# Early attention of a fused attention and two-FFN kernel: features taken from transposed queries, memory and normaliser in one product, and GpSimd given two elementwise jobs

## The chip, the cores and the metric

The kernel runs on one core of a Trainium2 chip. A core has TensorE (PE in the profile, with its weight loads on PEld), VectorE (DVE), ScalarE (ACT), GpSimd (POOL) and SyncE (SP), each with its own instruction queue, executed in order. Time is device microseconds (us) of one execution; three runs of the kernel before give a median of 1062.53 us.

## The reference

Causal attention over 4 batches of 8 heads (576 tokens, 64 columns a head) is mixed by a gate with a read from a linear memory; two feed-forward networks (FFNs) follow.

```python
a = softmax(causal(q @ k.T / sqrt(64)))            # per batch b and head h
local = a @ v
q_p = where(q > 0, q, exp(q) - 1) + 1              # the feature
mem_out = (q_p @ M_prev) / (q_p @ z_prev + 1e-6)
g = 1 / (1 + exp(-beta))
x = g * mem_out + (1 - g) * local                  # 2304 tokens x 512
h = x @ w_in                                       # 512 x 2048, layer 0
y = (max(h, 0) + log1p(exp(-abs(h)))) @ w_out
h = y @ w_in2                                      # layer 1
out = where(h > 0, h, exp(min(h, 0)) - 1) @ w_out2
```

## The kernel before

Tokens are cut into five chunks (`CHUNKS`) of 512 to 416. A chunk goes through layer 0 and then layer 1 in `ffn`: 16 steps f (a column block of 128 of the hidden layer), then 4 output blocks of 4 steps. Each fp32 product is made from two parts, a rounded high part and the rest as a low part (`hi`, `lo`; columns 0 and 1 of `x` and `g`), in three matmuls: hi x hi, hi x lo, lo x hi (L598 to L600 and L614 to L616). `convert` turns one raw 512 KB weight block into such a pair: ACT scales the upper words (L528), DVE shifts and joins the lower ones (L529, L530), ACT casts to the high part (L97, `w<-wr`), DVE subtracts to get the low part (L539). Raw blocks come through SP's queue into three buffers (tag `big`).

Attention is a generator. Part "A" is the first 256 tokens of a batch, part "B" the other 320; each is run head pair by head pair (4 pairs). A pair p of part "A" does: products of keys and queries (L294), mask and minimum on DVE (L333), exponentials on ACT (L338), the row scales on DVE (L348), transposes of the result (`group`, L373) and a copy to SBUF (L97, `pt<-tp`), and in `gather_pair` the product with the values (L407), summed in the PSUM bank `o` with the memory read (L404). `into` moves `o` into x: a cast on ACT (L142) and the low part on DVE (L143).

The memory read needs the feature. `feature` makes it with tokens on the partitions: exp (L241) and q+1 (L242) on ACT, then on DVE minimum and maximum (L243), a product with z (L244), a sum over the 64 columns (L246), gate and reciprocal (L249, L250) and the division (L252). `feature_t` transposes it on TensorE (L261) and ACT copies it back (L97, `phi<-tp`), so that L404 can multiply with M.

Part "A" of batches 0 and 1 fills chunk 0 and comes first, together with the first 14 weight blocks of layer 0 (`make(..., True)`); I call this the opening. Layer 0 of chunk 0 cannot begin before `x` of pair 0 of batch 1 is there. Afterwards `order` of `TUNE` says how many attention and conversion steps are called between FFN steps; parts "A" of batches 2 and 3 come first there. The order of instructions on each engine is decided when the program is built, by a scheduler with priorities, and is then fixed.

Of the kernel before, what the change touches and what calls it, by code (L numbers as in the profile page):

```python
# [23 lines left out]
TOK = ((128, 128), (0, 128), (512, 64), (384, 128), (256, 128))  # L24
# [34 lines left out]
def kernel(  # L59
# [32 lines left out]
    def f32(ap):  # L92
        return ap.bitcast(F32)
# [13 lines left out]
    iomg = const.tile([128, H], F32, name="iomg")  # L107

    def constants():
# [13 lines left out]
        ve.reciprocal(iomg, iomg)  # L123

# [20 lines left out]
    def attention(b, part, pool, early=None):  # L145
# [3 lines left out]
        cols = (1, 0) if first else (4, 3, 2)  # L149
# [16 lines left out]
        def load_kq(p):  # L166
# [3 lines left out]
            t = two.tile([128, 960], F32, name="kq", tag="kq")  # L170
# [12 lines left out]

        def load_rest(p):
            if first:
                if early:
                    for key in "qzvm":
                        d[key, p] = early[key][p]
                    return
                else:  # L190
                    t = (two if p % 2 else pool).tile([128, 6, 128], F32, name="ar", tag="ar")
                    ge.dma_start(t[:, 0:2, :], qz[b, p, :, 0:2, :])
                    ge.dma_start(t[:, 2, :], qz[b, p, :, 5, :])
                    ge.dma_start(
                        t[:, 3:5, :].rearrange("p h (t c) -> p h t c", t=2),
                        vm[b, p, :, 0:10, :].rearrange("p (h t) c -> p h t c", h=2)[:, :, 0:2, :],
                    )
                    ge.dma_start(t[:, 5, :].rearrange("p (h c) -> p h c", h=2), vm[b, p, :, 10:12, :])
                d["q", p], d["z", p] = t[:, 0:2, :], t[:, 2:3, :]
                d["v", p] = t[:, 3:5, :].rearrange("p h (t c) -> p h t c", t=2)  # L200
                d["m", p] = t[:, 5, :].rearrange("p (h c) -> p h c", h=2)
# [36 lines left out]
        def feature(p):  # L238
            q, z = d.pop(("q", p)), d.pop(("z", p))
# [15 lines left out]
        def feature_t(p):  # L255
            e = d.pop(("e", p))
# [6 lines left out]
            if plain:  # L263
                phi = two.tile([128, CB], F32, name="phi", tag="phi")
                copy(E[T["eva"][0]], phi[:, :n], pt[:, :n])
                d["phi", 2 * p] = d["phi", 2 * p + 1] = phi
                return
# [131 lines left out]
        def gather_pair(n):  # L399

            p = n // 2
            o = pso.tile([128, 512], F32, name="o", tag="o")
            for h in range(2):
                te.matmul(o[own(h), :w], d["vs", n + h][0][own(h)], d["phi", n + h][own(h), :w], start=True, stop=False)  # L404
            for j, p0, pn in ((0, 0, 256), (1, 256, 128)):
                for h in range(2):
                    te.matmul(o[own(h), :pn], d["vs", n + h][1][:, j, :], d["pt", n + h][0][:, p0:p0 + pn],  # L407
# [21 lines left out]
        if first:  # L429
            load_rest(1)  # L430
            load_rest(2)
        feature(0)
        prep_v(0)
        yield
        for p in range(NP if first else 0):
# [5 lines left out]
            if p + 2 < NP:  # L441
                load_kq(p + 2)
            yield
            if p:
                group(n - 2, d["pt", n - 2][0], ((1, 0), (0, 0), (1, 1)))
# [335 lines left out]
```

## Time and profile before

| what | before |
|---|---|
| median of 3 runs | 1062.53 us (1062.15 to 1063.73) |
| the profiled execution | 1062.3 us, span of its trace 1060.5 us |
| TensorE busy | 1029.0 us (97%) |
| DVE, ACT busy | 683.3 us (64%), 668.6 us (63%) |
| GpSimd busy | 91.4 us (9%) |

The span runs from the first to the last instruction; the 1.8 us between it and the execution's time lie outside the trace. TensorE's 97% is an average: its idle time is almost all in the first 90 us.

### The profile page before, as it was taken

Reading aid. Unit: us, or ns where it says so; the run is one execution under the profiler, and the core shown is the slowest. Engines: PE = TensorE matmul, PEld = TensorE weight load, DVE = VectorE, ACT = ScalarE, POOL = GpSimd, SP = SyncE. Lnnn points to the kernel's source line nnn. Section 1 sums busy time; section 2 is a strip of 40 time slices with the busy share of each in tenths; the row PEclk is TensorE's granted clock in tenths of the full one; section 3 lists DMA queues with packets and bytes.
Section 4 is the critical chain, followed back from the end, with each engine's and each line's share of the span. In section 5 each row is a group of like instructions: output and inputs, shape, how many; then the busy total and the mean of one; then the engine's idle time right before and its main releaser. Section 6 shows DMA issues by size and latency. Waiting matters only on the chain.

```text
span 1060.5 us, 15777 instructions
## 1 busy us (share of the span) xinstructions
PE 1029.0 (97%) x5328; PEld 904.7 (85%) x5328; DVE 683.3 (64%) x1698; ACT 668.6 (63%) x1458; POOL 91.4 (9%) x173
## 2 busy tenths in 40 slices
PE   7589999999999999999999999999999999999998
PEld 5356677788888888888889999999999999999998
DVE  6967799666768997897567756964675370240540
ACT  6759896697668977676569845654894350470330
POOL 7213330000000001000000000000000000000000
PEclk9989999999999999999999999999999999999999
DMA  9694489998976699646566466567545578777675
GB/s 284 185 367 147 149 274 329 336 332 293 336 279 246 220 311 343 207 165 193 198 228 235 170 233 217 178 231 241 194 162 176 182 247 246 247 234 233 231 235 174
DMA packets 73120, 251.65 MB, mean 237 GB/s; under 512 B 10320, under 2 KB 14928, under 8 KB 73040
## 3 DMA queue, kind: packets, MB, share of 16 engines
q1 hardware_dynamic: 64432, 216.56, 59.5%
q0 software_dynamic: 8608, 34.09, 10.1%
q8 instruction: 42, 0.69, 0.3%
q14 instruction: 38, 0.31, 0.1%
HBM read 212.34 MB, written 38.27 MB: 236 GB/s over the span
## 4 chain that ended last, share of the span: by engine, by line
PE 85%; DVE 6%; DMA 5%; ACT 2%; issue 1%; SPq 0%; ACTq 0%; DVEq 0%; POOLq 0%
PE h L614 12%; PE h L616 12%; PE h L615 12%; PE h L598 11%; PE h L600 11%; PE h L599 11%; PE tp L373 5%; PE o L388 2%; PE s L298 2%; PE h L298 2%; PE o L389 1%; PE o L407 1%; DMA w<-in_w1i 1%; PE s L294 1%; DVE wr L530 1%
## 5 line engine op out<-in xcount | busy, mean ns | idle before, releaser
L598 PE MATMUL h<-x,w 128*128 128x512 f32 (+2 forms) x640 | 238.5, 377 | 5.5 <-DVE t L577 2.3
L599 PE MATMUL h<-x,w 128*128 128x512 f32 (+2 forms) x640 | 239.6, 374 | 0.0
L600 PE MATMUL h<-x,w 128*128 128x512 f32 (+2 forms) x640 | 239.2, 374 | 0.0
L614 PE MATMUL h<-g,w 128*128 128x512 f32 (+2 forms) x640 | 238.4, 373 | 0.1
L616 PE MATMUL h<-g,w 128*128 128x512 f32 (+2 forms) x640 | 237.6, 372 | 0.0
L615 PE MATMUL h<-g,w 128*128 128x512 f32 (+2 forms) x640 | 237.3, 371 | 0.0
L598 PEld LDWEIGHTS h<-x,w 128*128 128x128 f32 x640 | 120.6, 189 | 21.1 <-DVE t L577 2.8
L600 PEld LDWEIGHTS h<-x,w 128*128 128x128 f32 x640 | 120.8, 189 | 13.4 <-issue 0.8
L599 PEld LDWEIGHTS h<-x,w 128*128 128x128 f32 x640 | 120.8, 189 | 12.5 <-issue 0.7
L614 PEld LDWEIGHTS h<-g,w 128*128 128x128 f32 x640 | 120.3, 188 | 12.8 <-issue 0.6
L616 PEld LDWEIGHTS h<-g,w 128*128 128x128 f32 x640 | 120.3, 188 | 11.9 <-issue 1.1
L615 PEld LDWEIGHTS h<-g,w 128*128 128x128 f32 x640 | 120.3, 188 | 11.7 <-issue 0.8
L603 DVE TENSOR_TENSOR g<-t,g 128x512 fp32r<-128x512 f32 (+2 forms) x160 | 101.0, 634 | 33.0 <-ACT g L602 31.5
L602 ACT CAST g<-t 128x512 fp32r<-128x512 f32 (+2 forms) x160 | 91.4, 573 | 24.6 <-DVE t L585 19.2
L321 ACT ACTIVATE sph<-sph,neg 128x384 f32<-128x384 f32 (+2 forms) x96 | 67.4, 702 | 31.9 <-DVE neg L315 31.4
L577 DVE SCALAR_TENSOR_TENSOR t<-h,t 128x512 f32<-128x512 f32 (+2 forms) x80 | 50.6, 636 | 57.2 <-ACT t L576 56.9
L379 DVE TENSOR_TENSOR ptb<-tp,ptb 128x512 fp32r<-128x512 f32 (+2 forms) x96 | 53.0, 575 | 38.2 <-ACT ptb L378 37.8
L378 ACT CAST ptb<-tp 128x512 fp32r<-128x512 f32 (+2 forms) x96 | 44.9, 498 | 46.4 <-PE tp L373 45.9
L373 PE MATMUL tp<-ident,sph 128*128 128x128 f32 x480 | 72.3, 282 | 1.5 <-ACT phi L97 1.1
L373 PEld LDWEIGHTS tp<-ident,sph 128*128 128x128 f32 x480 | 59.8, 145 | 9.8 <-ACT phi L97 1.5
L528 ACT ACTIVATE wr<-w 128x512 f32<-128x512 f32 x64 | 42.8, 669 | 35.0 <-DMA w<-in_w2i 11.7
L584 ACT ACTIVATE t<-t 128x416 f32<-128x416 f32 (+2 forms) x64 | 36.8, 579 | 41.4 <-DVE t L583 38.1
(117 smaller groups left out, 1535.3 us busy)
## 6 DMA issues: line engine op xcount, KB each, us to landing
w<-s_1i SPq DMA_DIRECT2D x79, 512.0 KB, 4.1
w<-s_0i SPq DMA_DIRECT2D x64, 512.0 KB, 4.2
w<-s_0o SPq DMA_DIRECT2D x64, 512.0 KB, 4.2
w<-s_1o SPq DMA_DIRECT2D x64, 512.0 KB, 4.2
qk<-in_qk POOLq DMA_DIRECT2D x32, 480.0 KB, 5.4
w<-in_w1i SPq DMA_DIRECT2D x16, 512.0 KB, 4.5
s_0i<-w SPq DMA_DIRECT2D x16, 512.0 KB, 7.0
w<-in_w1o SPq DMA_DIRECT2D x16, 512.0 KB, 5.3
```

What stands on the lines that cost most here:

```text
L321: se.activation(Pi, Pi, ACTF.Exp, scale=-1.0, bias=neg[:, i:i + 1], accum_out=sums(n, i))
L373: te.transpose(pt[:, c:c + 128], P[:, poff(n, i) + 128 * j:poff(n, i) + 128 * j + 128], ident)
L379: ve.tensor_sub(dst[:, 1, :c], pt[:, :c], f32(dst)[:, 0, :c])
L577: ve.scalar_tensor_tensor(t, h, 0.0, t, ALU.max, ALU.add)
L598: te.matmul(h[:, :N], hi[:, k, :], xk[:, 0, :N], start=k == 0, stop=False)
L599: te.matmul(h[:, :N], hi[:, k, :], xk[:, 1, :N], start=False, stop=False)
L600: te.matmul(h[:, :N], lo[:, k, :], xk[:, 0, :N], start=False, stop=k == KD - 1)
L602: se.copy(g[:, 0, :N], t[:, :N])
L603: ve.tensor_sub(g[:, 1, :N], t[:, :N], f32(g)[:, 0, :N])
L614: te.matmul(h[:, :N], hi[:, k, :], gs[f][:, 0, :N], start=f == 0, stop=False)
L615: te.matmul(h[:, :N], hi[:, k, :], gs[f][:, 1, :N], start=False, stop=False)
L616: te.matmul(h[:, :N], lo[:, k, :], gs[f][:, 0, :N], start=False, stop=f == KF - 1)
```

## The change

Batch parts "A" alone change; parts "B" and the FFNs keep their code.

- The feature is made from the transposed queries that lie beside the keys in `kq` already, for both heads of a pair at once, with no transpose ahead: exp on ACT, q+1 on GpSimd for batches 0 and 1 (`L258` of the new file) and on ACT for 2 and 3, minimum and maximum on DVE.
- One product per 128 tokens (L285) multiplies the feature with a 128 x 130 tile `mz`: M of both heads on the diagonal and two columns of z. Its PSUM result holds the memory read and the normaliser, tokens on the partitions. DVE adds, inverts (L289, L290) and scales (L292) it into `e`; `gather_pair` transposes `e` straight into the sum `o` (L438) ahead of the values' products.
- z comes once for all batches (`zc`, by one load and a transpose), M once a batch (`load_memory`); the per-pair loads of q, z and M fall away, and the values alone remain (one load a pair in place of four).
- The low part of the 14 early weight blocks is made by GpSimd (`ge.tensor_sub`) in place of DVE.
- The first three raw weight loads are issued between the first attention loads on SP's queue (`fetch`), and `kq` of pairs 2 and 3 of batch 1 gets buffers of its own.
- The two early 128-token tiles are stored in natural order, which only permutes rows and columns.

```diff
+    zc = const.tile([128, B * NP, 2], F32, name="zc")
...
+        nc.gpsimd.dma_start(zrow, qz[:, :, 0, 5, :].rearrange("b p c -> (b p) c"))
+        ge.memset(zc, 0.0)
+        te.transpose(zt[:, 0:B * NP], zrow, ident[0:B * NP, 0:B * NP])
+        for h in range(2):
+            ve.tensor_copy(zc[64 * h:64 * h + 64, :, h], zt[64 * h:64 * h + 64, 0:B * NP])
...
+        def load_memory():
+            t = pool.tile([128, NP, 130], F32, name="mz", tag="mz")
+            ge.memset(t, 0.0)
+            for h in range(2):
+                ge.dma_start(t[own(h), :, 64 * h:64 * h + 64], vm[b, :, own(h), 10 + h, :].rearrange("p r c -> r p c"))
+            ge.tensor_copy(t[:, :, 128:130], zc[:, b * NP:b * NP + NP, :])
...
         def feature(p):
+            if first:
+                q = d["kq", p][:, CA:2 * CA]
+                se.activation(e, q, ACTF.Exp)
+                if b < 2:
+                    ge.tensor_scalar(phi, q, 1.0, None, ALU.add)
+                else:
+                    se.activation(phi, q, ACTF.Identity, bias=ones)
+                ve.scalar_tensor_tensor(phi, e, 1.0, phi, ALU.min, ALU.max)
...
         def feature_t(p):
+            if first:
+                am = pss.tile([128, 512], F32, name="tp", tag="s")
+                for i in range(2):
+                    te.matmul(am[:, 130 * i:130 * i + 130], phi[:, 128 * i:128 * i + 128], d["mz"][:, p, :], start=True, stop=True)
+                ve.scalar_tensor_tensor(nrm, am[:, :, 128:130], 1e-6, g2, ALU.add, ALU.mult)
+                ve.reciprocal(nrm, nrm)
+                ve.tensor_mul(e, am, nrm.rearrange("p t (h o) -> p t h o", o=1).to_broadcast([128, 2, 2, 64]))
...
         def gather_pair(n):
-            for h in range(2):
-                te.matmul(o[own(h), :w], d["vs", n + h][0][own(h)], d["phi", n + h][own(h), :w], start=True, stop=False)
+            for i in range(2):
+                te.matmul(o[:, 128 * i:128 * i + 128], e[:, 128 * i:128 * i + 128], ident, start=i == 0, stop=False, is_transpose=True)
...
     def convert(src, key, w=None, later=False):
-            load = nc.sync.dma_start(w64.rearrange("p k n t -> p (k n t)"), src.bitcast(I32))
+            w64 = fetched.pop(key) if key in fetched else raw(src)
-        E[T["lo"]].tensor_sub(lo, wr, f32(hi))
+        (ge if later else ve).tensor_sub(lo, wr, f32(hi))
...
     def early_loads(pool):
-            nc.sync.dma_start(t, ar[p])
+            nc.sync.dma_start(t, ar[p, :, 3:5, :])
+            if p:
+                fetch(p - 1)
```

The line numbers move; L529, L530, L539, L243, L333, L348, L373, L407 and L598 of before are L579, L580, L589, L261, L366, L381, L406, L441 and L648 now.

The first place is DVE around the cast of batch 0's first pair into x. Here are twelve rows of before.

```order
L244 TENSOR_TENSOR ar_2_136<-e,ar_2_136 128x256
L243 SCALAR_TENSOR_TENSOR e<-e,ar_3_140 128x256
L529 TENSOR_SCALAR wr<-wr 128x512
L357 SCALAR_TENSOR_TENSOR sm<-sm,iomg 128x4
L143 TENSOR_TENSOR x_0_96<-o,x_0_96 128x256
L246 TENSOR_REDUCE nrm<-ar_2_136 128x4
L244 TENSOR_TENSOR ar_3_140<-e,ar_3_140 128x256
L539 TENSOR_TENSOR w<-wr,w 128x512
L530 SCALAR_TENSOR_TENSOR wr<-w_316,wr 128x512
L358 RECIPROCAL sm<-sm 128x4
L529 TENSOR_SCALAR wr<-wr 128x512
L249 SCALAR_TENSOR_TENSOR nrm<-nrm,ig 128x4
```

And these rows are DVE's of the change from the same cast (L151 now) on.

```order
L151 TENSOR_TENSOR x_0_97<-o,x_0_97 128x256
L381 TENSOR_SCALAR sph_95<-sph_95,sm 128x128
L381 TENSOR_SCALAR sph_95<-sph_95,sm 128x256
L381 TENSOR_SCALAR sph_96<-sph_96,sm 128x128
L381 TENSOR_SCALAR sph_96<-sph_96,sm 128x256
L579 TENSOR_SCALAR wr<-wr 128x512
L580 SCALAR_TENSOR_TENSOR wr<-w_351,wr 128x512
L579 TENSOR_SCALAR wr<-wr 128x512
L580 SCALAR_TENSOR_TENSOR wr<-w_394,wr 128x512
L261 SCALAR_TENSOR_TENSOR phi<-e,phi 128x256 x2
L289 SCALAR_TENSOR_TENSOR nrm<-tp,ig 128x4
L290 RECIPROCAL nrm<-nrm 128x4
```

The products with z, the sums and the subtractions of the weights have left the queue; the normaliser is read from PSUM (`tp`).

The second place is GpSimd's queue while the loads of batch 1 are issued; before, it held nothing but DMA issues there (`ar` is the tile of q, z, M and values, `kq` that of keys and queries).

```order
L192 DMA ar<-in_qz 128x256
L193 DMA ar<-in_qz 128x128
L194 DMA ar<-in_vm 128x2x128
L198 DMA ar<-in_vm 128x128
L173 DMA kq<-in_qk 64x256
L174 DMA kq<-in_qk 64x256
```

The corresponding stretch of the change follows.

```order
L197 MEMSET mz 128x520
L199 DMA mz<-in_vm 64x4x64 x2
L258 TENSOR_SCALAR phi<-kq 128x256
L200 COPY mz<-zc 128x4x2
L213 DMA ar<-in_vm 128x2x128 x2
L184 DMA kq<-in_qk 64x256
L589 TENSOR_TENSOR w<-wr,w 128x512
L185 DMA kq<-in_qk 64x256
L184 DMA kq<-in_qk 64x256
L185 DMA kq<-in_qk 64x256
L589 TENSOR_TENSOR w<-wr,w 128x512
```

Additions (L258) and subtractions (L589) now stand between the loads, so each waits for those ahead of it.

The third place is TensorE's queue up to layer 0's first product, first in the kernel before.

```order
L261 MATMUL tp<-ident,e 128x128 x2
L373 MATMUL tp<-ident,sph_94 128x128 x3
L373 MATMUL tp<-ident,sph_95 128x128 x3
L404 MATMUL o<-phi,ar 64x256 x2
L407 MATMUL o<-pt,ar 64x256 x2
L407 MATMUL o<-pt,ar 64x128 x2
L598 MATMUL h<-x_0_96,w 128x512 x4
```

The same place of the change reads as follows.

```order
L285 MATMUL tp<-mz,phi 128x130 x2
L406 MATMUL tp<-ident,sph_95 128x128 x3
L406 MATMUL tp<-ident,sph_96 128x128 x3
L438 MATMUL o<-ident,e 128x128 x2
L441 MATMUL o<-pt,ar 64x256 x2
L441 MATMUL o<-pt,ar 64x128 x2
L285 MATMUL tp<-mz,phi 128x130 x2
L406 MATMUL tp<-ident,sph_95 128x128 x3
L648 MATMUL h<-x_0_97,w 128x512 x4
```

As before, the last gather ahead of the FFN is that of batch 1's first pair; one feature product and half a group of transposes have moved ahead of L648.

## Rows read from the trace of the kernel before

**Rows 1.** Windows: stretch, length, then busy PE, PEld, DVE, ACT, POOL; clock; DMA.

```profile
0.00:63.06 63.06, 41.41 (x166) 27.55 (x166) 51.51 (x205) 44.91 (x130) 24.73 (x52) 0.89 0.78 249
63.06:85.20 22.14, 19.60 (x107) 13.20 (x107) 8.38 (x20) 10.02 (x22) 7.89 (x13) 1.00 1.02 393
85.20:200.00 114.80, 114.80 (x560) 83.70 (x561) 96.15 (x286) 92.17 (x226) 28.75 (x54) 0.99 0.66 226
```

**Rows 2.** Timeline where layer 0 begins: start, length, engine, line.

```profile
62.64 0.37 ACT L142 CAST x<-o 128x256 fp32r<-128x256 f32 x1 [1.04 <-PE o L407]
...
63.06 1.20 PE L598 MATMUL h<-x,w 128*128 128x512 f32 x4 [0.46 <-ACT x L142]
```

**Rows 3.** Windows of the opening in three parts, columns as in rows 1.

```profile
0.00:20.00 20.00, 13.52 (x43) 10.43 (x44) 11.88 (x65) 10.52 (x35) 14.46 (x34) 1.00 0.90 272
20.00:43.17 23.17, 14.41 (x56) 8.20 (x56) 21.43 (x71) 18.55 (x52) 5.96 (x11) 1.00 0.75 243
43.17:63.06 19.89, 13.48 (x69) 8.92 (x68) 18.20 (x69) 15.84 (x44) 4.31 (x8) 0.66 0.68 232
```

**Rows 4.** Waits from 0 to 63 us: total, times, longest.

```profile
PE tp L261 <- DVE e L252: 8.5, 3, 5.1
```

**Rows 5.** Chain that ended last, 26 to 30 us: start, length without overlap.

```profile
26.19 0.60 DVE wr L530
26.79 0.60 DVE w L539
27.39 0.94 DVE sph L348 x4
28.33 0.33 DVE ar L244
28.66 0.34 DVE e L243
29.00 0.34 DVE wr L529
...
29.66 0.40 DVE nrm L246
```

**Rows 6.** Lines by form, DVE, 0 to 82 us: count, busy, mean ns.

```profile
L539 DVE TENSOR_TENSOR w<-wr,w 128x512 fp32r<-128x512 f32 x14 | 9.5, 675 | 0.0
L244 DVE TENSOR_TENSOR ar<-e,ar 128x256 f32<-128x256 f32 x8 | 3.3, 417 | 0.0
```

**Rows 7.** Lines by form, ACT, 0 to 82 us.

```profile
L528 ACT ACTIVATE wr<-w 128x512 f32<-128x512 f32 x17 | 11.4, 671 | 12.7 <-DMA w<-in_w1i 9.7 <-DMA w<-in_w1o 2.1 <-DVE e L252 0.5
L97 ACT CAST w<-wr 128x512 fp32r<-128x512 f32 x14 | 8.7, 621 | 3.3 <-DVE wr L530 3.3
L242 ACT ACTIVATE ar<-ar,ones 128x256 f32<-128x256 f32 x8 | 4.1, 511 | 0.0
L241 ACT ACTIVATE e<-ar 128x256 f32<-128x256 f32 x8 | 3.4, 422 | 3.0 <-DMA ar<-in_ar 3.0
L97 ACT COPY phi<-tp 128x256 f32<-128x256 f32 x8 | 3.0, 369 | 2.7 <-PE tp L261 2.7
```

**Rows 8.** Timeline of TensorE, a pair at the full clock.

```profile
64.46 0.41 PE L261 MATMUL tp<-ident,e 128*128 128x128 f32 x2 [0.20 <-DVE e L252]
64.70 0.82 PE L373 MATMUL tp<-ident,sph 128*128 128x128 f32 x6
65.45 0.65 PE L404 MATMUL o<-phi,ar 64*64 64x256 f32 x4
66.03 0.50 PE L599 MATMUL h<-x,w 128*128 128x512 f32 x1
```

**Rows 9.** Lines, POOL, the whole span.

```profile
L173 POOL DMA_DIRECT2D kq<-in_qk x24 | 13.0, 541 | 29.1 <-PE h L294 18.4 <-PE s L294 10.7
...
L192 POOL DMA_DIRECT2D ar<-in_qz x12 | 7.0, 582 | 54.2 <-PE o L407 39.1 <-DVE nrm L246 7.2 <-issue 5.5
...
L690 POOL MEMSET ptb<- 128x384 f32 x1 | 0.4, 423 | 0.0
...
L111 POOL TENSOR_SCALAR_AFFINE_SELECT mask<-mask 128x128 f32<-128x128 f32 x1 | 0.3, 305 | 0.1
```

More of the change, by code (lines that the diff above doesn't have):

```diff
@@ L148, in attention @@
         tiles = (0, 1) if first else (2, 3, 4)
-        cols = (1, 0) if first else (4, 3, 2)
+        cols = (4, 3, 2)
         t0, nt = tiles[0], len(tiles)
@@ L169, in load_kq @@
                 return
-            t = two.tile([128, 960], F32, name="kq", tag="kq")
+            if first and b == 1 and p >= 2:
+                t = pool.tile([128, 512], F32, name="kq", tag="kq")
+            else:
+                t = two.tile([128, 960], F32, name="kq", tag="kq")
             for h in range(2):
@@ L186, in load_rest @@
                 if early:
-                    for key in "qzvm":
-                        d[key, p] = early[key][p]
+                    d["v", p] = early["v"][p]
                     return
-                else:
[L191 to L201, printed above, removed]
+                if p % 2 == (b < 2):
+                    t = two.tile([128, 6, 128], F32, name="ar", tag="ar")
+                else:
+                    t = pool.tile([128, 2, 128], F32, name="ar", tag="ar")
+                t = t[:, 0:2, :].rearrange("p h (t c) -> p h t c", t=2)
+                ge.dma_start(t, vm[b, p, :, 0:10, :].rearrange("p (h t) c -> p h t c", h=2)[:, :, 0:2, :])
+                d["v", p] = t
                 return
@@ L238, in feature @@
         def feature(p):
+            if first:
+                e = two.tile([128, 3, 128], F32, name="e", tag="e")[:, 0:2, :].rearrange("p t c -> p (t c)")
+                phi = two.tile([128, CB], F32, name="phi", tag="phi")[:, 0:CA]
+                q = d["kq", p][:, CA:2 * CA]
+                se.activation(e, q, ACTF.Exp)
+                if b < 2:
+                    ge.tensor_scalar(phi, q, 1.0, None, ALU.add)
+                else:
+                    se.activation(phi, q, ACTF.Identity, bias=ones)
+                ve.scalar_tensor_tensor(phi, e, 1.0, phi, ALU.min, ALU.max)
+                d["e", p], d["phi", p] = e, phi
+                return
             q, z = d.pop(("q", p)), d.pop(("z", p))
@@ L255, in feature_t @@
         def feature_t(p):
+            if first:
+                e, phi = d["e", p].rearrange("p (t h c) -> p t h c", t=2, h=2), d.pop(("phi", p))
+                am = pss.tile([128, 512], F32, name="tp", tag="s")
+                for i in range(2):
+                    te.matmul(am[:, 130 * i:130 * i + 130], phi[:, 128 * i:128 * i + 128], d["mz"][:, p, :], start=True, stop=True)
+                am = am[:, 0:260].rearrange("p (t c) -> p t c", t=2)
+                nrm = four.tile([128, 4], F32, name="nrm", tag="nrm").rearrange("p (t h) -> p t h", t=2)
+                g2 = ig[:, 2 * p:2 * p + 2].rearrange("p (t h) -> p t h", t=1).to_broadcast([128, 2, 2])
+                ve.scalar_tensor_tensor(nrm, am[:, :, 128:130], 1e-6, g2, ALU.add, ALU.mult)
+                ve.reciprocal(nrm, nrm)
+                am = am[:, :, 0:128].rearrange("p t (h c) -> p t h c", h=2)
+                ve.tensor_mul(e, am, nrm.rearrange("p t (h o) -> p t h o", o=1).to_broadcast([128, 2, 2, 64]))
+                return
             e = d.pop(("e", p))
@@ L262, in feature_t @@
                 n += r
[L263 to L267, printed above, removed]
             phi = [two.tile([128, CB], F32R, name="phi", tag="phi") for _ in range(2)]
@@ L440, in attention @@
             scores_pair(n)
-            if p + 2 < NP:
+            if p + 2 < NP and b != 1:
                 load_kq(p + 2)
@@ L518, in save, with fetch, raw @@
         E[T["st"]].dma_start(scratch[key], f32(w))
+    fetched = {}
+    def fetch(f):
+        key = f"0i{f}"
+        if wide and key not in fetched:
+            fetched[key] = raw(w1i[f])
+    def raw(src):
+        w64 = tri.tile([128, 4, 128, 2], I32, name="w64", tag="big")
+        load = nc.sync.dma_start(w64.rearrange("p k n t -> p (k n t)"), src.bitcast(I32))
+        raw_loads.append(load.ins)
+        return w64
     def convert(src, key, w=None, later=False):
@@ L632, in early_loads @@
     def early_loads(pool):
-        d = {key: [] for key in ("kq", "q", "z", "v", "m")}
+        d = {key: [] for key in ("kq", "v")}
         for p in range(NP):
```

41 lines of the change are left out of this document (22 added, 19 removed).

## The prediction

> **What bounds the kernel now.** I read the share of busy time by engine first, then windows around the point where layer 0 begins, then inside the first window the waits and the chain that ended last. After 63.06 us TensorE is the bound: it is busy 19.6 of 22.1 us and then 114.8 of 114.8 us, with DVE and ACT well below [rows 1]. The opening is another regime. TensorE is busy 41.4 of 63.06 us there, DVE 51.5, ACT 44.9, GpSimd 24.7. Layer 0's first product starts at 63.06 us, when ACT's cast of the second half of `x` of pair 0, begun at 62.64 us, is done [rows 2]. So what shortens the opening shortens the kernel, and what eases DVE or ACT later can give almost nothing.
>
> Inside the opening DVE is the busiest: 11.9 of 20 us at first, when loads and scores are only coming, then 21.4 of 23.2 and 18.2 of 19.9 us [rows 3]. TensorE's largest wait is for DVE's last feature step, 8.5 us in three waits [rows 4]. The chain of 26 to 30 us is almost all DVE, instruction after instruction: 0.60 us for joining a weight's words, 0.60 for its low part, 0.94 for four row scales, 0.33 for the product with z, 0.40 for the sum [rows 5]. These lengths are free of overlap, so I price DVE by them; the means of the records (0.675 us for the low part [rows 6]) overlap their neighbours.
>
> **The change, part by part, in the opening.**
>
> DVE. One of the 14 subtractions and one of the eight products with z lie behind 63.06 us, so 13 subtractions go, 13 x 0.60 = 7.8 us, and seven products and sums, 7 x (0.33 + 0.40) = 5.1 us. The minimum-maximum, the small steps and the division stay, the division now reading PSUM. The new order also lets fewer conversions ahead: on ACT ten of 14 scaling steps stand before the cast that starts layer 0, where all 14 stood; four shift-and-join pairs, 4 x (0.34 + 0.60) = 3.8 us [rows 5], are done after it, where DVE is busy only 8.4 of 22 us [rows 1]. Two small copies of z add some 0.2 us. DVE: 51.5 - 7.8 - 5.1 - 3.8 + 0.2 = 35.0 us.
>
> ACT. Eight additions of 1 go to GpSimd, 8 x 0.51 = 4.1 us; six copies of the transposed feature fall away, 6 x 0.37 = 2.2; four scalings, 4 x 0.67 = 2.7, four casts, 4 x 0.62 = 2.5, and one exponential, 0.4, come later [rows 7]. ACT: 44.9 - 11.9 = 33.0 us.
>
> TensorE. At the full clock a pair's two transposes take 64.70 - 64.46 = 0.24 us and its memory products 66.03 - 65.45 = 0.58 [rows 8]. Transposing `e` into `o` takes the same 0.24. The products with the 130-column tile are four records, as the four of the memory products are: at least four transpose records, (65.45 - 64.70) / 6 = 0.125 each, 0.50 us; at most four memory records, 0.58. So 0.74 to 0.82 us against 0.82: TensorE's 41.4 us stay.
>
> GpSimd. Twelve load issues fall away (three a pair, four pairs), 12 x 0.57 = 6.8 us, and five come (z, M twice two), 5 x 0.54 = 2.7 [rows 9]. Clearing two `mz` tiles costs 2 x 0.423 x 520/384 = 1.1 us. No row shows GpSimd with a two-input operation. A subtraction of 512 columns is bounded below by the memset, 0.423 x 512/384 = 0.56 us, above by four 128-column selects, 4 x 0.305 = 1.22 [rows 9]; I take 1.2, since the select also reads SBUF. By the same rows an addition on 256 columns is 0.28 to 0.61; I take 0.6. Nine subtractions and seven additions stand ahead of the last feature of batch 1: 10.8 + 4.2 = 15.0 us. GpSimd: 24.7 - 6.8 + 2.7 + 1.1 + 15.0 = 36.7 us. Behind each subtraction wait the loads of batches 1 and 2 and the later additions, for which DVE's minimum-maximum waits; with 36.7 us of work in about 50 this is cover enough. [...]
>
> SP. The loads of pairs 2 and 3 now stand behind one and two raw weight blocks of 512 KB, at 272 GB/s [rows 3] 1.9 us each. This is hidden by DVE's idle time in the first 20 us, 8.1 us [rows 3]; uncovered it costs up to 3.8 us. In return DVE and ACT get conversion work in that idle time.
>
> **The sum.** TensorE becomes the busiest engine of the opening with 41.4 us. The busiest one before filled 51.5 / 63.06 = 0.817 of it. I choose the same share, since the same queues in fixed order hold each other up: 41.4 / 0.817 = 50.7 us. For GpSimd and DVE in each other's way I add 1.0 (next part). Layer 0 then starts at 51.7 us, 11.4 us earlier. After that TensorE has the same work; eight pairs of batches 2 and 3 save 0 to 8 x 0.08 = 0.6 us, of which I take 0.3. The profiled execution would fall from 1062.3 by 11.7 to 1050.6 us; the median of before lies 0.2 above its profiled execution, so I predict **1050.8 us**. A difference below 0.2% (2.1 us) is about what cannot be told from no change.
>
> **Does GpSimd stop DVE?** No row shows a GpSimd operation on tensors beside a busy DVE, so the price lies between nothing and the whole of GpSimd's 15.0 us added to DVE's. The reason for 1.0 is that DVE would be idle for 51.7 - 35.0 = 16.7 us and need not have been working then. [...]
>
> **The rivals.**
>
> 1. *Likeliest, 0.63:* the opening ends at 47 to 56 us, the time is 1046 to 1055, as above.
>
> 2. *DVE is held up, 0.14.* All 15.0 us of GpSimd's tensor work come on top of DVE's 35.0: 50.0 us, at the share of 0.817 an opening of 61.2 us. The gain is 1.9 + 0.3, the time 1060.3; with two thirds of it, 1056. For it: joins and low parts were back to back, so a held join holds all behind it. Against: GpSimd is idle or issuing loads most of the time.
>
> 3. *The waits vanish too, 0.13.* TensorE's largest wait was for DVE, which loses a third of its work. With TensorE never waiting the opening is 41.4 us and the time 1040; half-way, at 45 us, it is 1044. For it: the conversions start in idle time, and the transpose-copy hop is gone. Against: one bank `o` serves all gathers, each of which waits for the cast and subtraction of the one before.
>
> 4. *Slower, 0.05:* GpSimd's in-order queue becomes the bound. Its work without subtractions is 36.7 - 10.8 = 25.9 us, so nine subtractions fill the old opening if one takes (63.06 - 25.9) / 9 = 4.1 us. From there on layer 0, whose product with the low part waits for GpSimd, starts later; at 4.5 us a subtraction, it starts at 66.4 and the time is 1065.6. Against: that is over three times the upper bound from rows.
>
> 5. *The opening shrinks but nothing is gained, 0.05.* From 63.06 to 85.20 us the DMA engines are full (share 1.02, 393 GB/s [rows 1]) with saves and the next weights. If that traffic and not TensorE ends this stretch, and does not move ahead since four raw blocks are still to come, the time stays at 1062.5. Against: TensorE is idle only 2.5 us there.
>
> **How the numbers follow.** The likeliest case gives 1050.8. The range reaches into rivals 2 and 3, as far as a blocked share of two thirds to three quarters on one side and an opening of 44 us on the other: 1043 to 1058.8 us; outside it are the rest of rival 2, the end of 3, and 4 and 5. Faster by over 0.2%: cases 1 and 3 and most of 2, 0.63 + 0.13 + 0.12 = 0.88. Within 0.2%: 5 and the end of 2, 0.07. Slower: 0.05.
>
> **What the profile after would show.** L648's first product near 52 us, after a cast into the second half of `x` of pair 0; TensorE the busiest of the opening, DVE near 35 us busy. L589 near 1.2 us a piece and DVE's joins (L580) still near 0.60: if these grow to 1 us and more beside L589, rival 2 holds. From L648 on, the same 997 us to the end. Wrong I would be if TensorE waits for GpSimd at L285 or L650, if its idle time after layer 0's start grows beyond 5 us, or if the row scales and joins stretch.

## The result, and the profile after

The changed kernel takes 1075.15 us (median of 4 runs, 1069.34 to 1077.68), the kernel before 1062.81 beside it: a ratio of 1.0102, 95% interval [1.008, 1.0124]. I had predicted 1050.8 us, in a range of 1043 to 1058.8. The change is slower, by 12 us, and the sign was wrong.

The profiled execution of the changed kernel took 1076.27 us, its span is 1074.5 us. Its windows, in the columns of [rows 1]:

```profile
0.00:63.20 63.20, 37.81 (x176) 29.42 (x177) 45.59 (x170) 35.80 (x108) 41.97 (x67) 0.81 0.57 167
63.20:85.20 22.00, 18.23 (x100) 13.11 (x98) 11.61 (x24) 13.50 (x30) 13.86 (x17) 1.00 0.93 368
85.20:200.00 114.80, 113.68 (x566) 88.53 (x566) 90.72 (x260) 90.69 (x212) 18.12 (x32) 0.99 0.78 269
200.00:220.00 20.00, 14.21 (x56) 9.89 (x56) 12.73 (x28) 12.89 (x26) 2.72 (x6) 0.81 0.90 312
220.00:240.00 20.00, 20.00 (x83) 16.32 (x82) 15.04 (x30) 18.12 (x34) 1.08 (x2) 0.93 0.81 298
240.00:262.00 22.00, 16.62 (x67) 13.17 (x66) 12.46 (x24) 16.80 (x31) 0.00 (x0) 0.92 0.63 205
```

And the kernel before, in the part that the prediction had no rows for:

```profile
200.00:220.00 20.00, 18.86 (x81) 14.73 (x80) 12.62 (x22) 16.15 (x30) 0.00 (x0) 1.00 0.99 364
220.00:240.00 20.00, 19.93 (x86) 15.89 (x85) 13.41 (x22) 18.41 (x33) 0.54 (x1) 1.00 0.91 321
240.00:262.00 22.00, 21.42 (x102) 17.59 (x101) 14.99 (x30) 17.39 (x33) 0.54 (x1) 1.00 0.81 283
```

Two things are to be seen. The opening is as long as it was: layer 0's first product starts at 63.20 us against 63.06. VectorE is less busy there (45.6 us against 51.5 [rows 1]), but TensorE is busy only 37.8 of the 63.2 us. And from 200 to 262 us, where TensorE was busy 60.2 us, it is now busy 50.8 us, at a granted clock of 0.81, 0.93 and 0.92 in the three windows, where it was 1.00 in each. The span behind the opening is 1074.5 - 63.2 = 1011.3 us against 997.4: that is the whole loss.

What TensorE waits for from 180 to 270 us in the changed kernel (total, times, longest):

```profile
PE h L648 <- DVE t L627: 4.8, 1, 4.8
PE h L648 <- ACT x L150: 2.9, 1, 2.9
PE h L648 <- DMA w<-s_0i: 2.8, 1, 2.8
```

The middle line leads to the attention: chunk 1's first layer waits for its own input. The timeline of the changed kernel shows batch 2's first feature product, the first product of chunk 1, its wait, and the last cast of chunk 1's `x`:

```profile
104.56 0.61 PE L285 MATMUL tp<-mz,phi 128*128 128x130 f32 x4
187.66 0.40 PE L648 MATMUL h<-x,w 128*128 128x512 f32 x1
204.33 1.20 PE L648 MATMUL h<-x,w 128*128 128x512 f32 x4 [2.94 <-ACT x L150]
207.76 0.37 ACT L150 CAST x<-o 128x256 fp32r<-128x256 f32 x1 [1.54 <-PE o L441]
```

The same places in the timeline of the kernel before:

```profile
92.44 0.38 PE L261 MATMUL tp<-ident,e 128*128 128x128 f32 x2
193.31 0.38 ACT L142 CAST x<-o 128x256 fp32r<-128x256 f32 x1 [1.59 <-PE o L407]
201.06 0.40 PE L598 MATMUL h<-x,w 128*128 128x512 f32 x1
```

Before, the last `x` was there 7.8 us ahead of chunk 1's first product. Now that product starts 13.4 us earlier and the last `x` comes 14.5 us later, 20.1 us behind it. TensorE had run ahead with chunk 0's FFN, and the attention of batches 2 and 3 came after it. This is in the order in which TensorE's instructions are written: of the 64 first-term products of chunk 0's layer 0 (L598, L648), 24 stood ahead of batch 2's first feature step, and 40 do in the changed kernel. I call this number the **place**.

What ended the waits themselves is another matter. Before two of the three, the 2.9 and the 4.8 us, ScalarE stood still for a raw weight block of layer 1, and what TensorE needed stood behind that block's scaling (L578) in ScalarE's queue:

```profile
202.98 0.66 ACT L578 ACTIVATE wr<-w 128x512 f32<-128x512 f32 x1 [3.59 <-DMA w<-in_w2i]
203.90 0.38 ACT L150 CAST x<-o 128x256 fp32r<-128x256 f32 x1
254.65 0.66 ACT L578 ACTIVATE wr<-w 128x512 f32<-128x512 f32 x1 [4.75 <-DMA w<-in_w2i]
255.21 0.71 ACT L626 ACTIVATE t<-t,ones 128x512 f32<-128x512 f32 x1
256.41 0.68 DVE L627 SCALAR_TENSOR_TENSOR t<-h,t 128x512 f32<-128x512 f32 x1
257.15 0.80 PE L648 MATMUL h<-x,w 128*128 128x512 f32 x1 [4.83 <-DVE t L627]
```

The third wait is for a stored weight block read back. From 63 to 310 us ScalarE waited 26.5 us for raw blocks of layer 1 in the changed kernel and 11.6 us in the kernel before. So the late attention can be one part of the loss, and raw weights that came late for ScalarE another; no run below separates the two.

GpSimd and VectorE in the opening, from the lines by form of the changed kernel (count, busy, mean ns):

```profile
L589 POOL TENSOR_TENSOR w<-wr,w 128x512 fp32r<-128x512 f32 x9 | 11.7, 1305 | 9.4 <-ACT w L97 7.6 <-DVE phi L261 1.7
L258 POOL TENSOR_SCALAR phi<-kq 128x256 f32<-128x256 f32 x8 | 7.7, 958 | 2.4 <-PE tp L285 2.3
L580 DVE SCALAR_TENSOR_TENSOR wr<-w,wr 128x512 int32<-128x512 int32 x10 | 8.3, 834 | 0.1
L381 DVE TENSOR_SCALAR sph<-sph,sm 128x256 f32<-128x256 f32 x16 | 6.8, 425 | 0.0
L381 DVE TENSOR_SCALAR sph<-sph,sm 128x128 f32<-128x128 f32 x16 | 6.3, 392 | 0.1
```

And of the kernel before:

```profile
L530 DVE SCALAR_TENSOR_TENSOR wr<-w,wr 128x512 int32<-128x512 int32 x14 | 9.6, 682 | 0.0
L348 DVE TENSOR_SCALAR sph<-sph,sm 128x256 f32<-128x256 f32 x16 | 5.6, 348 | 0.0
L348 DVE TENSOR_SCALAR sph<-sph,sm 128x128 f32<-128x128 f32 x16 | 4.5, 279 | 0.0
```

Some of VectorE's operations took longer where GpSimd worked beside them. The timeline of the changed kernel shows when: four row scales take 1.00 us where the next subtraction begins only at their end (23.61 us), and 2.02 us beside one; a join (0.60 us [rows 5]) grows to 2.15 us.

```profile
19.16 2.02 DVE L381 TENSOR_SCALAR sph<-sph,sm 128x128 f32<-128x128 f32 x4
19.64 1.38 POOL L589 TENSOR_TENSOR w<-wr,w 128x512 fp32r<-128x512 f32 x1 [2.14 <-ACT w L97]
22.79 1.00 DVE L381 TENSOR_SCALAR sph<-sph,sm 128x128 f32<-128x128 f32 x4
52.61 2.15 DVE L580 SCALAR_TENSOR_TENSOR wr<-w,wr 128x512 int32<-128x512 int32 x1
52.92 1.28 POOL L589 TENSOR_TENSOR w<-wr,w 128x512 fp32r<-128x512 f32 x1
54.16 1.30 POOL L258 TENSOR_SCALAR phi<-kq 128x256 f32<-128x256 f32 x1
```

The join ends at 54.76 us, 0.56 us after the subtraction, and the addition that begins meanwhile takes 1.30 us, where the mean of the eight is 0.96. What made them longer no row shows. Over the opening the means give, for joins and row scales alone, 10 x 0.15 + 16 x 0.08 + 16 x 0.11 = 4.5 us. The joins' part is that single one: the other nine took 0.68 to 0.69 us. Shifts (514 ns against 416), the minimum-maximum (548 against 418) and a small step on 128 x 4 (L390, 293 against 156) add 1.0 + 0.9 + 1.1, some 7.5 us in all.

### The profile page after: what moved, and what is told of

Its sections match the earlier page's. It is cut to its first block, busy times and chain, and to the rows that moved or that the text cites. A ratio compares the mean times of both kernels' runs of the same rounds, so it can differ in the third digit from the quotient of the medians.

```text
span 1074.5 us, 15752 instructions
## 1 busy us (share of the span) xinstructions
PE 1025.7 (95%) x5329; PEld 911.8 (85%) x5329; DVE 678.2 (63%) x1654; ACT 662.5 (62%) x1434; POOL 106.8 (10%) x177
## 4 chain that ended last, share of the span: by engine, by line
PE 77%; DMA 10%; DVE 6%; ACT 4%; issue 2%; SPq 1%; ACTq 0%; DVEq 0%
PE h L664 11%; PE h L665 11%; PE h L666 11%; PE h L648 10%; PE h L649 10%; PE h L650 10%; PE tp L406 4%; DMA w<-in_w2i 3%; DMA w<-in_w1i 3%; DMA s_1i<-w 3%; PE o L421 2%; PE s L331 2%; PE h L331 1%; PE o L422 1%; DVE wr L580 1%
## 5 line engine op out<-in xcount | busy, mean ns | idle before, releaser
L648 PE MATMUL h<-x,w 128*128 128x512 f32 (+2 forms) x640 | 238.7, 379 | 15.7 <-DVE t L627 7.2
L648 PEld LDWEIGHTS h<-x,w 128*128 128x128 f32 x640 | 121.5, 190 | 31.2 <-DVE t L627 11.4
L627 DVE SCALAR_TENSOR_TENSOR t<-h,t 128x512 f32<-128x512 f32 (+2 forms) x80 | 50.5, 635 | 63.5 <-ACT t L626 63.2
L406 PE MATMUL tp<-ident,sph 128*128 128x128 f32 x480 | 72.4, 282 | 0.8 <-DVE neg L366 0.4
L578 ACT ACTIVATE wr<-w 128x512 f32<-128x512 f32 x64 | 42.6, 669 | 49.2 <-DMA w<-in_w2i 26.8
L406 PEld LDWEIGHTS tp<-ident,sph 128*128 128x128 f32 x480 | 59.6, 145 | 9.6 <-DVE sph L381 1.3
```

The lines of the kernel that those rows point to most:

```text
L406: te.transpose(pt[:, c:c + 128], P[:, poff(n, i) + 128 * j:poff(n, i) + 128 * j + 128], ident)
L627: ve.scalar_tensor_tensor(t, h, 0.0, t, ALU.max, ALU.add)
L648: te.matmul(h[:, :N], hi[:, k, :], xk[:, 0, :N], start=k == 0, stop=False)
```

## The experiments

Theories at first: A, GpSimd's queue, with the subtractions in it, holds up the attention of batches 2 and 3; B, GpSimd's work only slows VectorE; C, the new feature path, or the raw weight loads that it puts ahead of the keys. The table gives for each run the first product of layer 0 (opening), batch 2's first feature step (b2), and layer 1's first product, in us of the one execution that was profiled; then the median and its ratio to the kernel before, run on the same chip.

| run | place | opening | b2 | layer 1 | median us | ratio, 95% interval |
|---|---|---|---|---|---|---|
| before | 24 | 63.1 | 92.4 | 304.1 | 1062.8 | 1 |
| after | 40 | 63.2 | 104.6 | 317.5 | 1075.2 | 1.0102 [1.008, 1.0124] |
| e1 | 24 | 68.7 | 94.4 | 308.3 | 1067.0 | 1.0015 [0.9998, 1.0031] |
| e2 | 24 | 61.6 | 92.3 | 304.5 | 1063.9 | 0.9985 [0.997, 1.0001] |
| e3 | 48 | 55.4 | 104.8 | 306.0 | 1066.5 | 1.0003 [0.999, 1.0016] |
| e4 | 40 | 64.7 | 110.1 | 327.2 | 1074.3 | 1.0066 [1.0042, 1.0089] |
| e5 | 24 | 70.1 | 102.5 | 311.9 | 1071.1 | 1.0068 [1.0047, 1.0089] |
| e6 | 40 | 61.2 | 102.7 | 306.8 | 1070.8 | 1.006 [1.0038, 1.0082] |
| e7 | 40 | 60.4 | 98.6 | 305.8 | 1064.5 | one run |
| e8 | 24 | 64.1 | 93.9 | 301.0 | 1061.4 | 0.9986 [0.997, 1.0002] |
| e9 | 40 | 60.6 | 103.3 | 315.2 | 1074.5 | 1.0083 [1.0055, 1.011] |
| e10 | 24 | 64.1 | 93.1 | 304.0 | 1063.3 | 1.0002 [0.9991, 1.0014] |
| e11 | 47 | 62.1 | 107.5 | 313.8 | 1074.9 | 1.0105 [1.0087, 1.0123] |
| e12 | 30 | 65.0 | 100.2 | 311.2 | 1070.7 | 1.0053 [1.0032, 1.0075] |
| e13 | 24 | 53.9 | 82.9 | 300.0 | 1059.9 | 0.9958 [0.9937, 0.998] |
| e14 | 28 | 71.4 | 104.5 | 318.8 | 1080.1 | 1.0148 [1.0114, 1.0182] |
| e15 | 24 | 59.3 | 88.9 | 303.2 | 1062.7 | 0.9992 [0.9977, 1.0007] |
| e16 | 32 | 64.6 | 97.5 | 303.8 | 1062.5 | 0.9989 [0.9974, 1.0003] |

From layer 1's start to the end of the span it is 756 to 758 us in all of these but e4, so each difference is made before it. In e4 it is 747.4 us: its faster pace brings 51 more matmul records of the attention ahead of layer 1, so that its 327.2 us can't be set beside the others. Executions of one kernel lie up to 9 us apart (e6: 1066.1, the profiled one, to 1075.6 us), so a few us between two rows of the profiled columns decide nothing by themselves.

**e1, e2, e3: one part each.** In e1 the subtraction goes back to VectorE:

```diff
-        (ge if later else ve).tensor_sub(lo, wr, f32(hi))
+        ve.tensor_sub(lo, wr, f32(hi))
```

> The changed kernel with the 14 early weight tiles' subtraction (L589) back on VectorE; everything else of the change stays. Theory A (GpSimd's queue): the subtractions, which wait for ACT's casts, stand ahead of the loads and of the memory tile of batches 2 and 3 on GpSimd's queue, so the attention of these batches falls behind the FFN, and chunk 1 starts without its x. Then the feature product of batch 2's first pair comes back from 104.6 us to 92 to 97 us, TensorE's busy time in 200 to 400 us rises from 187 to 196 us or more, and the time falls to 1058 to 1065 us, though VectorE has 14 x 0.675 = 9.5 us more to do in the opening. Theory B (only VectorE's stretched operations count): the opening loses the 7.5 us of stretch, gains 9.5 us of work, so about 65 us to the first product, and nothing changes behind it: 1075 to 1078 us. Theory C (the new feature path itself holds up batches 2 and 3): TensorE still idles at 200 to 260 us; 1072 to 1078 us.

e2 is e1 with two more edits, which leave the feature rewrite alone:

```diff
-            if p:
-                fetch(p - 1)
...
-                if b < 2:
-                    ge.tensor_scalar(phi, q, 1.0, None, ALU.add)
-                else:
-                    se.activation(phi, q, ACTF.Identity, bias=ones)
+                se.activation(phi, q, ACTF.Identity, bias=ones)
```

> The changed kernel with the subtraction on VectorE, q + 1 on ScalarE for all batches, and no raw weight load moved ahead: the transposed features with memory and normaliser in one product alone. Theory A: no loss behind the opening, keys arrive early as before, VectorE has about 44 us of work in the opening instead of 51.5, so the first product of layer 0 comes at 56 to 61 us and the time is 1055 to 1061 us. Theory C (feature path itself holds up batches 2 and 3): 1068 to 1078 us, with TensorE idle at 200 to 260 us as in the changed kernel. Third possibility, that the opening is set by the pace of raw loads and casts: first product at 62 to 64 us, 1061 to 1065 us.

e3 is the kernel before with the subtraction alone on GpSimd:

```diff
-        E[T["lo"]].tensor_sub(lo, wr, f32(hi))
+        (ge if later else ve).tensor_sub(lo, wr, f32(hi))
```

> The kernel before with one edit alone: the subtraction of the 14 early weight tiles on GpSimd. Theory A: the attention of batches 2 and 3 falls behind (in program order the first feature transposes of batch 2 come after 48 of layer 0's 64 first-term products instead of 24), chunk 1 waits for x, TensorE idles 8 to 14 us more between 190 and 270 us; the opening gains 0 to 4 us; time 1066 to 1077 us. Theory B: VectorE is relieved of 9.5 us and stretched by 5 to 8 us, the first product of layer 0 comes at 59 to 64 us, nothing changes behind: 1058 to 1064 us. Theory C (the new feature path is what loses): 1058 to 1063 us.

With the subtraction on VectorE the loss is gone (e1), though the opening is 5.5 us longer. The feature rewrite alone is worth nothing that can be measured (e2). So C falls as the cause of the loss. e3 shortens the opening by 7.7 us and gives all of it back behind it, in windows where the kernel before had 50.00 of 50 us busy from 100 to 150 us:

```profile
62.00:100.00 38.00, 32.31 (x141) 23.78 (x140) 21.96 (x36) 27.23 (x52) 14.59 (x19) 0.96 0.89 331
100.00:150.00 50.00, 47.25 (x240) 34.60 (x239) 46.30 (x148) 45.68 (x117) 17.65 (x32) 1.00 0.75 250
```

**e4: more attention per FFN step.**

```diff
-    order=((0, 0, (1.6, 0.0), (0.6, 0.2)), ...
+    order=((0, 0, (2.2, 0.0), (0.6, 0.2)), ...
```

> The changed kernel with one number: during chunk 0's first half of layer 0 the schedule gives the attention of batches 2 and 3 a share of 2.2 steps per FFN step instead of 1.6, so that its last gather comes behind 64 of layer 0's products instead of 76. The GpSimd queue stays as it is. If the loss is the place in the order: TensorE's idle time at 190 to 270 us falls from 14 us to 3 to 6 us and the time is 1064 to 1069 us. If the loss is that GpSimd's queue delivers batch 2 late whatever the order says: the first feature product of batch 2 stays at 104 to 105 us, the idle time moves to 100 to 190 us, and the time is 1072 to 1080 us.

The second case, by the time and the idle time, which moves forward; b2 comes later still, and the place is 40 as before. The windows of e4 show 38.0 - 30.2 = 7.8 and 50.0 - 44.1 = 5.9 us idle where the changed kernel had 4.5 and 0.4:

```profile
62.00:100.00 38.00, 30.20 (x144) 22.54 (x143) 18.15 (x36) 23.45 (x47) 14.96 (x19) 0.90 0.82 310
150.00:200.00 50.00, 44.13 (x229) 31.20 (x227) 41.84 (x139) 35.96 (x96) 8.65 (x16) 0.97 0.68 226
```

So a faster pace did not buy back the late start here. In one point theory A was mistaken: in e1 the loads of the memory tiles of batches 2 and 3 are issued by 88 us, in the changed kernel by 85 us. The queue of GpSimd did not bring them later; the written order used them later.

**e5 to e8: the place.** e5 changes a priority in the changed kernel:

```diff
-                with tc.high_priority(offset=400):
+                with tc.high_priority(offset=3000):
```

> The changed kernel with one number: the priority of the attention steps of batches 2 and 3 against the FFN, 3000 instead of 400. Nothing moves between engines, GpSimd keeps all 14 subtractions. In TensorE's written order the first feature product of batch 2 then stands behind 24 first-term products of layer 0 instead of 40, as it does in the kernel with the feature rewrite alone, and the last gather behind 70 instead of 76. Theory A in its new form (the written order, which a scheduler sets from its own estimate, lets the FFN run ahead of the attention): batch 2's first feature product runs at 91 to 97 us instead of 104.6, layer 1 starts at 303 to 309 us instead of 317.5, and the time is 1060 to 1067 us, with the opening as long as in the changed kernel (63 us). Theory A in its old form (the queue on GpSimd delivers late) and theory B (GpSimd's work slows VectorE): the product waits for its data, layer 1 still starts at 314 us or later, 1070 to 1078 us.

e6 and e7 are e2 with the subtraction of some tiles on GpSimd; e8 is e7 with e5's edit:

```diff
-        ve.tensor_sub(lo, wr, f32(hi))
+        (ge if later and len(made) < 4 else ve).tensor_sub(lo, wr, f32(hi))    # e6
+        (ge if later and len(made) % 2 else ve).tensor_sub(lo, wr, f32(hi))    # e7, e8
```

> The feature rewrite alone (q + 1 on ScalarE, no raw load moved ahead), with the subtraction of only the first 4 of the 14 early tiles on GpSimd. That is some 5.4 us of GpSimd's time, all early; but in TensorE's written order the first feature product of batch 2 stands behind 40 first-term products instead of 24. If the written order decides: opening 59 to 62 us, layer 1 starts at 309 to 317 us, time 1066 to 1074 us. If the amount of GpSimd's work decides: as the feature rewrite alone or a little better, 1059 to 1064 us.

> The feature rewrite alone, with the subtraction of every second of the early tiles on GpSimd and the priority of the attention at 400; the first feature product of batch 2 stands behind 40 first-term products. Written order: opening 57 to 61 us, layer 1 starts at 309 to 317 us, 1066 to 1074 us. Amount of GpSimd's work: 1056 to 1063 us.

> As the kernel that alternates the subtraction between VectorE and GpSimd, with the attention's priority at 3000: the first feature product of batch 2 stands behind 24 first-term products instead of 40. Written order: the opening is as short as in that kernel (57 to 61 us) and nothing is lost behind it: layer 1 starts at 297 to 302 us and the time is 1053 to 1060 us, better than both the kernel before and the changed one. Otherwise the same time as that kernel.

From opening to layer 1, e5 takes 241.8 us where the changed kernel took 254.3, and e8 236.9 where e7 took 245.5. Part of that was paid in the opening, 6.9 and 3.7 us, and both missed the times that the written order gave, e5 by 4 us, e8 by 1.4. In e5 the reason is in its timeline. Loads had gone ahead of the constants, and GpSimd made the mask only at 7.42 us. The first mask step came 9 us later still: two conversions stood ahead of it in VectorE's queue, the second waiting for ScalarE and a raw block. TensorE stood still meanwhile.

```profile
7.42 0.34 POOL L113 TENSOR_SCALAR_AFFINE_SELECT mask<-mask 128x128 f32<-128x128 f32 x1
15.75 0.56 DVE L579 TENSOR_SCALAR wr<-wr 128x512 int32<-128x512 int32 x1 [4.08 <-ACT wr L578]
16.35 0.69 DVE L580 SCALAR_TENSOR_TENSOR wr<-w,wr 128x512 int32<-128x512 int32 x1
16.96 0.42 DVE L366 CUSTOM_DVE_ANT_0 sph<-h,mask 128x256 f32<-128x256 f32 x1
17.65 7.96 PE L327 MATMUL h<-kq 64*128 64x256 f32 x28 [8.07 <-DVE neg L366]
```

Four subtractions on GpSimd, 5 us of work, are enough to move the place to 40 and lose 0.6% (e6): not the amount of GpSimd's work decides. Against the place stands e7, a single run: seven subtractions, the same place of 40, and 1064.5 us, under the 1066 to 1074 that the written order gave.

**e9, e10, e11: the other parts.** e9 is the changed kernel without `fetch` (e2's first edit). e10 is e9 with e1's edit. e11 is e2 with all 14 subtractions on GpSimd.

> The changed kernel without the three raw weight loads that it issues among the first loads; TensorE's written order stays (batch 2's first feature product behind 40 first-term products of layer 0). Theory C (raw loads ahead of the keys delay the opening): TensorE's wait for the keys falls from 9.9 us to 3 to 5 us, the first product of layer 0 comes at 56 to 60 us instead of 63.2, layer 1 starts at 310 to 315 us, and the time is 1068 to 1072 us; the loss behind the opening stays. If the wait for the keys is only replaced by the next one (VectorE's queue): opening 62 to 64 us, 1072 to 1077 us.

> The changed kernel without the raw loads moved ahead and with the subtraction on VectorE: the feature rewrite with the early q + 1 on GpSimd. It stands between two kernels that ran: with q + 1 on ScalarE too, opening 61.6 us and 1063.9 us; with the raw loads ahead, opening 68.7 us and 1067.0 us. If the raw loads ahead of the keys cost those 7.1 us: opening 60 to 63 us, 1061 to 1064 us. If q + 1 on GpSimd costs them (0.96 us each instead of 0.3 on ScalarE, and a place in GpSimd's queue behind loads): opening 66 to 69 us, 1066 to 1069 us.

> The feature rewrite alone, with the subtraction of all 14 early tiles on GpSimd: no raw load ahead, q + 1 on ScalarE. In TensorE's written order batch 2's first feature product stands behind 47 first-term products. Against the feature rewrite alone (opening 61.6 us, layer 1 at 304.5 us, 1063.9 us) my own prediction would have its gain: VectorE has 9.5 us less, opening 53 to 58 us. The written order then takes it back: 248 to 256 us from there to layer 1, which starts at 304 to 312 us, time 1062 to 1071 us. If nothing is taken back: 1055 to 1059 us.

The raw loads ahead of the keys lengthened the opening by 2.6 us, as TensorE's wait for the keys shows (9.9 us with them, 5.6 without), but not the kernel. q + 1 on GpSimd costs nothing that can be measured in the time (e10), though the opening of 64.1 us missed its range by 1.1; and on ScalarE it takes 0.50 us (e2; 0.51 in the kernel before [rows 7]), not the 0.3 that I had put there, which no run shows. e11, with neither, is as slow as the changed kernel: **the subtraction on GpSimd, together with the new feature path, is the whole loss.** Behind the opening the subtraction costs about the same on either feature path: 250.6 us to layer 1 in e3 against 241.0 in the kernel before, 251.7 in e11 against 242.9 in e2. The two paths differ in the opening, where e3 gains 7.7 us and e11, against its expectation, nothing. Its opening is no shorter than e2's, though VectorE is busy 43.48 us of the first 62 where it was 49.77. The first row is e11's window, the timeline under it shows row scales, 1.00 us for four when alone, beside the subtractions:

```profile
0.00:62.00 62.00, 42.09 (x169) 32.33 (x169) 43.48 (x166) 37.24 (x113) 31.59 (x57) 0.92 0.56 153
```

```profile
22.26 3.51 DVE L378 TENSOR_SCALAR sph<-sph,sm 128x128 f32<-128x128 f32 x4
22.47 1.27 POOL L586 TENSOR_TENSOR w<-wr,w 128x512 fp32r<-128x512 f32 x1 [3.28 <-ACT w L97]
24.34 1.27 POOL L586 TENSOR_TENSOR w<-wr,w 128x512 fp32r<-128x512 f32 x1
```

**e12, e13, e14: the place with the constants first.** Two numbers each, in the changed kernel (e12), in e3 (e13) and in e9 (e14). The attention's priority is 6000 in all three; the 1000 in the expectation of e12 is not what ran.

```diff
-        with tc.high_priority(offset=1000):
+        with tc.high_priority(offset=6000):
             constants(pre)
...
-                with tc.high_priority(offset=400):
+                with tc.high_priority(offset=6000):
```

> The changed kernel with two numbers: the priority of the attention steps of batches 2 and 3 is 1000 instead of 400, and that of the constants 6000 instead of 1000, so that they stay first. The first feature product of batch 2 stands behind 30 of layer 0's first-term products instead of 40. Written order: opening 61 to 66 us, 240 to 246 us from there to layer 1, which starts at 303 to 309 us instead of 317.5; time 1060 to 1067 us. If the place is only a companion of another cause (the subtractions on GpSimd themselves): 250 us or more from the opening to layer 1, time 1070 us or more.

> The kernel before with the subtraction of the 14 early tiles on GpSimd, and the same two priorities: the first feature transpose of batch 2 stands behind 24 first-term products instead of 48. Written order: the opening stays near 55.4 us (to 59 us), 238 to 244 us from there to layer 1, which starts at 295 to 302 us; time 1052 to 1060 us, faster than the kernel before. If the subtractions on GpSimd cost what they give: layer 1 at 304 to 308 us, 1062 to 1068 us.

> The changed kernel without the raw loads moved ahead, with the same two priorities: place 28 instead of 40. Written order: opening 58 to 63 us, 238 to 244 us to layer 1, which starts at 298 to 306 us; 1055 to 1064 us. Otherwise as without the priorities: 254 us from the opening to layer 1, 1071 to 1076 us.

e12 gives back half: 246.2 us from the opening to layer 1 instead of 254.3, the ratio falls from 1.0102 to 1.0053, but it misses the time expected of the written order. e13 is faster than both kernels, 0.9958 [0.9937, 0.998], 4.5 us, with an opening of 53.9 us; it too loses something behind it (246.1 us). e14 went against the expectation: b2 at 104.5 us, since its opening of 71.4 us grew by 10.7, for a reason that was not traced. So the place alone doesn't order the runs; the time at which batch 2's attention starts does better, since it holds the opening as well. Over the 17 kernels, e4 left out, the correlation with layer 1's start, worked out from the table, is 0.79 for b2, 0.49 for the opening and 0.40 for the place.

**e15, e16: no subtraction at all.** In e2 and in the kernel before, the low part of the 14 tiles is not made, and the high part stands in for it, so that the output is another:

```diff
+        if not later:
+            ve.tensor_sub(lo, wr, f32(hi))
...
+            return w[:, 0], w[:, 0]
```

> The feature rewrite alone, with the subtraction of the 14 early tiles left out on every engine: their low part is not made, and the high part stands in for it in the products and in the copy that is saved, so the output is another. VectorE has 14 x 0.675 = 9.5 us less, GpSimd has nothing more, and batch 2's first feature product stands behind 24 first-term products as in the feature rewrite alone. If GpSimd's interference ate the gain: opening 52 to 56 us against 61.6, time 1054 to 1058 us. If VectorE's amount of work does not set the opening: 59 to 62 us, 1060 to 1064 us.

> The kernel before with the same left out. With the subtractions on GpSimd its opening was 55.4 us (63.1 with them on VectorE). If interference cost something there too: 51 to 54 us; if not: 54.5 to 56.5 us. Behind the opening, with batch 2 behind 32 first-term products, 240 to 246 us to layer 1; time 1052 to 1060 us.

Both are as fast as the kernel before, within the intervals. The opening is 59.3 us in e15 and 64.6 us in e16, though VectorE has 9.5 us less to do and GpSimd nothing more:

```profile
0.00:62.00 62.00, 45.27 (x191) 34.25 (x192) 44.36 (x184) 44.77 (x129) 22.28 (x50) 0.97 0.80 256
```

So VectorE's amount of work alone does not set the opening, each kernel in its own written order. And the 7.7 us that e3 gained there can't be VectorE's relief alone either: e16 has the same relief, was expected at 51 to 56.5 us, and opens 9.2 us later than e3. The order in which the queues are written differs between the two; that it makes the 9.2 us is not shown.

## Why the prediction was wrong

The step that failed, as the prediction put it, is "After that TensorE has the same work", and from it "From L648 on, the same 997 us to the end". The work is the same, its order is not. The subtraction on GpSimd moved the attention of batches 2 and 3 from 24 to 40 products into layer 0; batch 2 starts 12.1 us later and layer 1 13.4 us later, and e1, e2 and e11 show that the subtraction does it. That it does it through the place is in part argued, since the place alone orders the runs badly. The raw weights of layer 1 are the rival: ScalarE's wait for them, 26.5 us, is 24.3 in e9 and 17.0 in e11, which lose like the changed kernel, and 3.1 in e1 and 11.7 in e2, which don't. But e7 has 17.1, and no run changed this wait alone. TensorE's idle time from the start of layer 0 to 262 us grew from 4.3 to 16.1 us; the prediction had 5 us as its sign of being wrong. I had read the written order only at the opening, and the place stood in it.

Step by step:

- **The opening, 51.7 us forecast, 63.2 measured.** "TensorE becomes the busiest engine of the opening" and the share of 0.817 failed: VectorE stayed the busiest, TensorE was busy 0.60 of it. e15 shows that taking 9.5 us from VectorE moves the opening by 2.3 us. So VectorE's sum does not set it; a chain through queues in fixed order is what I take to set it, which was not traced. A term of 11.4 us was read from sums of busy time. TensorE's wait for the feature, which was to shrink with VectorE's work, grew from 8.5 us [rows 4] to 10.4 us:

```profile
PE tp L285 <- DVE phi L261: 10.4, 3, 5.1
```

- **VectorE 35.0, measured 45.6 us.** The stretched operations account for some 7.5 us; the rest is open. The stretch that I had named as a sign of being wrong came, in the means of the row scales. That of rival 2, joins of 1 us and more, came in one join of ten, and the mean is 834 ns against 682. But the two engines' meeting is no price of the opening's length that I can give: e15, without any subtraction, opens 2.8 us before e11, which has all of them on GpSimd, and their written orders differ too. Of the 1.0 us that I took for it, no run gives the right size.
- **GpSimd 36.7, measured 42.0 us.** A subtraction took 1.31 us where I took 1.2, above my upper bound of 1.22; the addition on 256 columns took 0.96, above my upper bound of 0.61, because a select's length was scaled by columns.
- **The raw loads ahead of the keys**, "up to 3.8 us" uncovered: TensorE's waits for the keys grew from 4.6 to 9.9 us, and without them the opening is 2.6 us shorter (e9). The opening's part lies within that size, the cover was not there, and the kernel's time shows nothing of it.
- **Rival 5** had the gain handed back, by DMA traffic from 63 to 85 us. The DMA share fell from 1.02 [rows 1] to 0.93 there, and the loss came later. **Rivals 1, 3 and 4** fall with the opening; GpSimd's subtraction is far from 4.1 us. That the change came out slower, for which I gave 0.05 to rival 4, was not by rival 4's way.
- **The range.** Two of its sums don't come out. Two thirds of 15.0 us on VectorE give an opening of 45.0 / 0.817 = 55.1 us and 1054.2 us, not 1056; and 1058.8 us is a blocked share of nine tenths. Put right, they would not have held the measured time either.

What stays open: why subtractions in GpSimd's queue make the scheduler write batch 2 later was not traced. How much of the 13.4 us is the place alone is not settled: e12 returned 6.3 of them and e5 5.6, each with an opening that moved as well. And what ends the opening at 54 to 71 us in kernels with nearly the same work was shown not to be VectorE's amount of work alone, but its chain was not taken apart.

## What to carry to other kernels

An operation that moves to another engine's queue can move whatever a scheduler places by its own estimate, here also 100 us further on: follow the written order on the bounding engine to the next hand-over of data, not only at the place of the edit, and compare when each producer starts there. Ask also what stands ahead of that producer in its own queue, and what it waits for. A busy share of 0.8 did not make VectorE the bound of this opening of short dependent steps: ask first what the time would be with the work left out, as e15 does. When work goes to GpSimd, price it against VectorE's scales and joins beside it as a meeting, not as free capacity: here four scales took 2.02 us beside a subtraction where they took 1.00 without, and one join 2.15 us where nine took 0.68 to 0.69.

## What the runs showed of the hardware

- In the opening of the changed kernel GpSimd's single-input addition on 128 x 256 took 0.96 us (mean of eight), its two-input subtraction on 128 x 512 1.31 us (mean of nine): with half the columns and one input less the time was a quarter shorter.
- Row scales on VectorE, with one tensor input, took 2.02 us for four beside one subtraction of GpSimd (changed kernel), 3.51 us beside two (e11), and 1.00 us without. A step on 128 x 4, L390, whose mean was 0.16 us in the kernel before (L357 there), took 1.24 us beside one (at 23.70 us).
- TensorE's granted clock was 1.00 in the kernel before from 200 to 262 us. In the changed kernel, where TensorE was idle 5.8 of 20 and 5.4 of 22 us, it was 0.81 and 0.92 in those windows, and 0.93 in the fully busy window between them.
